# Attention and two layer pairs on one core: bias rows and transposes for two heads at a time, with a new order of the work

## The chip, the cores and the metric

The kernel runs on one core of a Trainium2 chip. Its engines are TensorE (PE, matmuls; PEld is its weight load), VectorE (DVE), ScalarE (ACT), GpSimd (POOL) and SyncE (SP), which here issues every DMA. The metric is the device time of one execution in microseconds (us); lower is better. The kernel before took 1053.97 us in the median of three runs (1053.57 to 1055.98).

## The reference

Batch 4, 8 heads, 576 positions, head size 64. The scores get a bias per head from a small network on the distance of two positions; softmax and the value product follow. The result, 2304 tokens of 512, goes through two layer pairs of 512 to 2048 to 512.

```python
scores = scale * np.matmul(q, k.transpose(0, 1, 3, 2))
x = (psi_rel / psi_i)[..., None]
bias = np.maximum(x @ w1 + b1, 0.0) @ w2            # one row per position and head
scores = scores + bias.transpose(2, 0, 1)[None]
attn = np.exp(scores - np.max(scores, axis=-1, keepdims=True))
attn = attn / (np.sum(attn, axis=-1, keepdims=True) + 1e-09)
x = np.matmul(attn, v)                              # then tokens x 512
h = x @ w_in; x = (s * np.maximum(h, 0.0) ** 2 + b) @ w_out
h = x @ w_in2; return (h - np.tanh(h)) @ w_out2
```

## The kernel before

**Precision.** Operands of the large matmuls are split into a high and a low f16 part, and three products are taken. So most data pass through a pair of steps: a copy to f16 ("hi") and the rest ("lo"). Layer weights of eight bytes are first converted by three VectorE instructions (L1253, L1256, L1259).

**Attention.** A unit is one head of 128 query rows of one batch, or two heads of the last 64 rows; there are 144, in groups of four that share an accumulator. For each unit (`unit_tasks`, `unit_rest`): one matmul group makes the scores of two heads (L1041); VectorE adds the bias row tile `bi` and takes the maximum (L1073); a small addition makes the exponent's offset (`mx_add`, L1081); ScalarE takes the exponential and its sum (L1087); `hi` copies it to f16 (L1099 on ScalarE, L1097 on VectorE); `lo` makes the low part in two pieces (`lo_a`, `lo_b`, L1104); a DMA transpose moves the 128 x 1152 tile `hl` into the 9 blocks of `et` (L1119); `pv` multiplies with the values (L1132, L1138). `x_tasks` scales a finished group and transposes it into the first layer's input (L1217, four blocks; L1220 for 64 rows).

**Bias.** For each of 36 blocks Q of 16 positions (`bias_tasks`) four hidden tiles are made (`hid`, L727 on ScalarE, L730 else; GpSimd only for Q < `QG`, which is 7), multiplied (L761), evacuated in two pieces into a tile of the `et` ring (`out`, L611, L615) and written to DRAM (`btd`). `bias_rows` reads them back skewed, one transfer for each head, into `bi`. Two batches share a load.

**Rings.** Each kind of tile has a fixed number of slots, handed out in order: `bi` 4, `hl` 3, `et` 4 (for heads and for bias rows on their way out), each for one head.

**Layers.** The first pair works on blocks of 256 tokens (`moe1_in`, L1573, L1645) from the moment four groups are through, beside the rest of attention. When attention is done (`turn`), its memory goes to the second pair's weights, which are converted, combined and split (L1852, L618) while TensorE works off the first pair; then the second pair runs (L2038, L2166).

**The order.** A planner (`Schedule.forward`) simulates engines and one DMA queue and emits the instructions in the order found. Each task has costs for the engines that may do it. `COST` multiplies them by kind, `XFER` scales transfers and gives their delay, `ENGINE` ties a task of a stage or group to engines (keys `u0` to `u9` are groups of four units), `SHIFT` moves its priority. `PORT` and `share` say whether it is kept from running beside GpSimd.

Of the kernel before, what the change touches and what calls it, by code (L numbers as in the profile page):

```python
# [8 lines left out]
F32 = mybir.dt.float32  # L9
F16 = mybir.dt.float16  # L10
# [16 lines left out]
SHARE0, QP, QA, SCU, QG = 21, 8, 16, 12, 7  # L27
# [3 lines left out]
AHEAD = 6.97  # L31
COST = {
    "u.ex@act": 0.848, "u.hi@act": 0.904, "bias.lambda@act": 1.1, "f.relu@act": 0.952, "f.square@act": 1.15,
    "x.lambda@act": 1.2, "w.lambda@act": 1.13, "scan.sq@act": 1.17, "bias.out@act": 1.0315, "f.out@act": 1.1149,
    "w.square@act": 1.07, "k.hi@act": 1.15, "s.lambda@act": 1.09, "q.hi@act": 1.2, "v.hi@act": 1.14,
    "u.ttr@dve": 0.84944, "f.hi@dve": 1.152216, "u.hi@dve": 0.87312, "s.in_done@dve": 1.1143, "scan.add@dve":
    0.8125, "f.lambda@dve": 1.174, "s.out_done@dve": 1.662, "u.lo@pool": 0.9991, "f.lo@pool": 0.782085,
    "bias.lambda@pool": 1.0466, "u.qk@pe": 0.885, "u.pv@pe": 0.97, "u.tr@sp": 1.04, "x.lambda@sp": 1.083,
    "q.fn@sp": 1.36, "J.c@dve": 1.2701, "J.fn@dve": 1.12, "L.lambda@dve": 1.0069, "L.square@act": 0.919,
    "P.wsum@dve": 1.0042, "X.scales@dve": 0.7943, "X.sums@dve": 1.21, "X.xsum@dve": 1.1245, "bias.lambda@dve":  # L40
    1.0453, "bias.out@dve": 1.179, "f.norm@dve": 1.2446, "f.out@dve": 1.0696, "f.scales@dve": 0.4404,
    "k.hi@dve": 1.1296, "k.lambda@dve": 1.047, "q.hi@dve": 1.1098, "s.lambda@dve": 1.0224, "scan.lambda@dve":
    0.857, "v.hi@dve": 1.738, "v.lambda@dve": 1.0251, "w.lambda@dve": 0.993, ".begin@dve": 0.784, ".lambda@dve":
    1.116, "L.scales@dve": 0.961, "L.sums@dve": 0.868, "X.lambda@act": 1.021, "X.lambda@dve": 1.023,
    "q.lambda@dve": 1.026, "w.scale_out@dve": 0.859, "u.lo@act": 0.97, "u.lo_a@act": 0.97, "u.lo_b@act": 0.97,
    "u.lo@dve": 0.97, "u.lo_a@dve": 0.97, "u.lo_b@dve": 0.97, "u.lo_a@pool": 0.97, "u.lo_b@pool": 0.97,
    "f.lo@act": 0.85, "f.lo@dve": 0.85, "f.hi@act": 1.04, "f.hi@pool": 1.04, "u.hi@pool": 0.8, "u.ex@dve": 0.8,
    "u.ex@pool": 0.8, "u.ttr@act": 0.8, "u.ttr@pool": 0.8,
}
XFER = {  # L50
    "bias.fn": (0.79893, 1.75), "f.fn": (1.5147, 1.23), "k.fn": (1.07019, 1.73), "q.fn": (1.05633, 1.81),
    "scan.fn": (0.80982, 2.01), "u.fn": (1.21869, 1.21), "u.tr": (1.0197, 2.23), "v.fn": (0.97218, 2.27),
    "w.fn": (0.91872, 2.03), "x.fn": (1.188, 1.54), "x.lambda": (0.81873, 1.51), "L.fn": (0.87714, 2.6), "J.fn":
    (0.33264, 1.52), "X.fn": (1.54341, 1.41), "o.fn": (0.8514, 0.99), ".fn": (0.78903, 1.4),
# [10 lines left out]
    "dve", "u12.lo_a": "pool", "u12.lo_b": "pool", "u13.lo_a": "pool", "u13.lo_b": "pool", "u17.lo_b": "pool",  # L65
# [12 lines left out]
    "act", "X7.lambda": "act", "x5.hi": "dve", "x12.hi": "dve", "I3.lambda": "act", "u1.lo_b": "pool",  # L78
# [4 lines left out]
    "dve", "X3.lambda": "dve",  # L83
# [4 lines left out]
    ".begin": 158.6, ".eye": 204.2, ".fn": -49.3, ".lambda": 60.6, "I0.add": 1197.4, "I0.fn": -551.5,  # L88
# [324 lines left out]
def tile_kernel(  # L413
# [318 lines left out]
    def bias_tasks(Q):  # L732
# [1594 lines left out]
```

## Time and profile before

| | us |
|---|---|
| median of 3 runs | 1053.97 |
| profiled execution | 1057.96 |
| its span | 1056.2 |
| TensorE busy | 964.1 (91%) |
| VectorE busy | 881.6 (83%) |
| ScalarE busy | 667.5 (63%) |
| GpSimd busy | 250.1 (24%) |

The span runs from the first to the last instruction; the profiled execution's own time is 1.8 us longer. Shares of busy time are means over stages that have different limits: GpSimd works in the first 600 us alone, and TensorE is at 99% in the last third. Matmuls overlap one another in the trace, so the busy time of TensorE is no measure of its peak. Where a line is a helper's, such as L468 (plain DMAs) or L618 (low parts), the tile names tell the step.

### The profile page before, as it was taken

Reading aid. Unit: us, or ns where it says so; the run is one execution under the profiler, and the core shown is the slowest. Engines: PE = TensorE matmul, PEld = TensorE weight load, DVE = VectorE, ACT = ScalarE, POOL = GpSimd, SP = SyncE. Lnnn points to the kernel's source line nnn. Section 1 sums busy time; section 2 is a strip of 40 time slices with the busy share of each in tenths; the row PEclk is TensorE's granted clock in tenths of the full one; section 3 lists DMA queues with packets and bytes.
Section 4 is the critical chain, followed back from the end, with each engine's and each line's share of the span. In section 5 each row is a group of like instructions: output and inputs, shape, how many; then the busy total and the mean of one; then the engine's idle time right before and its main releaser. Section 6 shows DMA issues by size and latency. Waiting matters only on the chain.

```text
span 1056.2 us, 32450 instructions
## 1 busy us (share of the span) xinstructions
PE 964.1 (91%) x13486; PEld 833.2 (79%) x13486; DVE 881.6 (83%) x1918; ACT 667.5 (63%) x1307; POOL 250.1 (24%) x319
## 2 busy tenths in 40 slices
PE   5676678999988999999997999988999999999998
PEld 3233356778767788788886888878999999999998
DVE  6999899876568677786774889999999999999885
ACT  4797659749767565776853687766554555464452
POOL 6146437247542334455511000000000000000000
PEclk9767679899999999999999999998999999999999
DMA  9969995899999879999896904410001100100000
GB/s 341 398 227 216 311 236 119 184 200 252 245 197 230 168 179 176 201 188 207 171 180 104 397 21 138 148 36 12 32 23 32 52 23 22 42 22 23 22 22 22
DMA packets 261444, 153.66 MB, mean 145 GB/s; under 512 B 197680, under 2 KB 229552, under 8 KB 261296
## 3 DMA queue, kind: packets, MB, share of 16 engines
q1 hardware_dynamic: 261296, 151.59, 59.1%
q8 instruction: 105, 1.72, 0.7%
q14 instruction: 43, 0.35, 0.1%
HBM read 84.03 MB, written 20.33 MB: 99 GB/s over the span
## 4 chain that ended last, share of the span: by engine, by line
PE 43%; DVE 9%; ACT 3%; DMA 2%; issue 2%; POOL 1%; SPq 0%; DVEq 0%; ACTq 0%; POOLq 0%
PE acc L2166 14%; PE pa L2038 9%; PE pb L2038 7%; PE po L1645 5%; PE ph L1573 4%; PE po L2166 2%; DMA et<-hl 2%; DVE w2big L1852 2%; DVE w2big L618 1%; PE sp L1041 1%; DVE w1big L618 1%; ACT e L1087 1%; POOL hl L1104 1%; PE xp L1132 1%; DVE hr L1603 1%
## 5 line engine op out<-in xcount | busy, mean ns | idle before, releaser
L1645 PE MATMUL po<-hr,w1big 128*128 128x256 f16 x1728 | 202.9, 274 | 3.6 <-ACT x L1664 2.7
L1104 POOL TENSOR_TENSOR hl<-e,hl 128x64 f16<-128x64 f32 (+1 forms) x200 | 160.2, 818 | 184.9 <-ACT hl L1099 107.2
L1573 PEld LDWEIGHTS <-w1big 128*128 128x128 f16 x1728 | 166.9, 99 | 31.5 <-issue 10.6
L1645 PEld LDWEIGHTS <-w1big 128*128 128x128 f16 x1728 | 165.5, 98 | 26.5 <-issue 7.1
L2038 PEld LDWEIGHTS <-w2big 128*128 128x128 f16 x3024 | 175.2, 99 | 2.2 <-issue 2.1
L2166 PEld LDWEIGHTS <-w1big 128*128 128x128 f16 x3024 | 172.8, 98 | 0.0
L1087 ACT ACTIVATE e<-sp,mx 128x576 f32<-128x576 f32 x144 | 105.6, 735 | 70.3 <-POOL mx L1081 34.3
L1073 DVE CUSTOM_DVE_ANT_0 sp<-sp,bi 128x576 f32<-128x576 f32 x144 | 107.0, 772 | 20.2 <-PE sp L1041 16.2
L1573 PE MATMUL ph<-xt_own,w1big 128*128 128x256 f16 x960 | 113.1, 274 | 3.0 <-ACT r L1586 2.2
L1041 PE MATMUL sp<-ks,qs 64*128 64x288 f16 (+1 forms) x960 | 84.2, 296 | 25.8 <-ACT e L1087 24.8
L1573 PE MATMUL ph<-w1big 128*128 128x256 f16 x768 | 91.2, 276 | 3.3 <-ACT r L1586 2.6
L1041 PEld LDWEIGHTS <-qs 64*128 64x128 f16 (+1 forms) x960 | 48.7, 99 | 53.0 <-issue 42.2
L1132 PEld LDWEIGHTS <-et 128*128 128x128 f16 (+1 forms) x1440 | 54.7, 104 | 41.2 <-issue 21.5
L1132 PE MATMUL xp<-vp,et 128*128 128x64 f16 (+1 forms) x1440 | 65.4, 199 | 19.1 <-DMA et<-hl 11.7
L2166 PE MATMUL acc<-hr,w1big 128*128 128x128 f16 x1296 | 79.9, 219 | 0.0
L1099 ACT ACTIVATE hl<-e 128x576 f16<-128x576 f32 x96 | 64.7, 678 | 23.1 <-DMA et<-hl 20.2
L2166 PE MATMUL acc<-w2big,w1big 128*128 128x128 f16 x1296 | 79.0, 219 | 0.0
L1104 DVE TENSOR_TENSOR hl<-e,hl 128x512 f16<-128x512 f32 (+1 forms) x88 | 48.8, 572 | 15.9 <-ACT hl L1099 13.0
L2038 PE MATMUL pa<-w1big,w2big 128*128 128x128 f16 x960 | 59.9, 219 | 1.7 <-ACT w2big L2057 0.9
L1586 ACT ACTIVATE r<-ph 128x512 f32<-128x512 f32 x72 | 42.3, 590 | 25.8 <-PE ph L1573 21.3
L1591 ACT ACTIVATE r<-r,sq 128x512 f32<-128x512 f32 x72 | 51.2, 718 | 0.9
L2074 ACT ACTIVATE w1big<-w1big 128x512 f32<-128x512 f32 x34 | 21.3, 630 | 45.6 <-DVE w1big L2064 33.4
(229 smaller groups left out, 1757.7 us busy)
## 6 DMA issues: line engine op xcount, KB each, us to landing
bi<-btd SPq DMA_DIRECT2D x64, 288.0 KB, 4.1
w1big<-in_wout SPq DMA_DIRECT2D x12, 1024.0 KB, 6.0
btd<-et SPq DMA_DIRECT2D x36, 295.5 KB, 3.7
w1big<-in_win SPq DMA_DIRECT2D x8, 1024.0 KB, 9.7
w2big<-in_win SPq DMA_DIRECT2D x8, 1024.0 KB, 13.1
x2d<-x SPq DMA_DIRECT2D x36, 128.0 KB, 3.1
w1big<-x2d SPq DMA_DIRECT2D x36, 128.0 KB, 2.3
outT<-xt_own SPq DMA_DIRECT2D x18, 256.0 KB, 2.2
```

What stands on the lines that cost most here:

```text
L1041: nc.tensor.matmul(out=out, lhsT=qs.tile[64 * h:64 * h + 64, sq, p * r:p * r + r], rhs=ks.tile[64 * h:64 * h + 64, sk, half * HS:(half + 1 ...
L1073: nc.vector.tensor_tensor_reduce(out=st, in0=st, in1=bi.tile.rearrange("p (a b) -> p a b", a=2), scale=-1.0 / KAP, scalar=3.0e38, op0=ALU. ...
L1087: nc.scalar.activation(out=put(e, row_tile("e")).rearrange("p (a b) -> p a b", a=2), in_=sp.tile[:, :, 0:HS], func=AF.Exp, scale=-1.0, bia ...
L1099: nc.scalar.activation(out=h[:, 0:S], in_=e.tile, func=AF.Copy)
L1104: eng_of(eng).tensor_tensor(out=hl.tile[:, o:o + m], in0=e.tile[:, c:c + m], in1=hl.tile[:, c:c + m], op=ALU.subtract)
L1132: nc.tensor.matmul(out=xp[r0:r0 + r, o:o + 64], lhsT=et.tile[:, n, r0:r0 + r], rhs=vp.tile[:, 0, n % 5, 64 * h:64 * h + 64], start=n == 0, ...
L1573: nc.tensor.matmul(out=ph.tile[:, fi, :], lhsT=win_ap(1, sw, m, f), rhs=xa(sx, m), start=m == 0 and j == 0, stop=m == KM - 1 and j == 2,)
L1586: nc.scalar.activation(out=r.tile, in_=ph.tile, func=AF.Relu)
L1591: nc.scalar.activation(out=r.tile, in_=r.tile, func=AF.Square, scale=sq[:, fp // 4:fp // 4 + 1])
L1645: nc.tensor.matmul(out=po.tile[:, :NB1], lhsT=wout_ap(1, sw, f, c), rhs=rhl[f // 8][:, f % 8, sr, :], start=f == 0 and j == 0, stop=f == K ...
L2038: nc.tensor.matmul(out=bank.tile[:, f * HT:(f + 1) * HT], lhsT=w[:, sw, m, f * 128:(f + 1) * 128], rhs=xs[:, sx, m], start=p in (1, 2, 5) ...
L2166: nc.tensor.matmul(out=bank.tile[:, o + c * HT:o + (c + 1) * HT], lhsT=w[:, sw, f, c * 128:(c + 1) * 128], rhs=g[:, sx, f], start=new and ...
```

## The change

- Bias rows: `bi` holds two heads, one transfer loads both (for 64 rows two transfers, each with one half of two units); the ring has 2 slots.
- Exponentials: `hl` and `et` hold two heads, rings of 2 slots. The transpose is issued once for a pair, 18 blocks, when the low parts of both are done; both value products follow it.
- Two bias blocks share one `et` slot, each with its own write to DRAM; the second's evacuation comes after the first's.
- Further engines: `mx_add` on ScalarE, relu of the first pair and the four-bank copies `E` of the second pair on VectorE, `hid` on GpSimd for all Q (`QG` 36).
- The identity for the weight norm's maximum and the maximum are two-byte.
- `COST`, `XFER`, `ENGINE`, `SHIFT` and some planner constants have new values, by which the order of all engines changes. An entry of `ENGINE` may name several engines.

```diff
-SHARE0, QP, QA, SCU, QG = 21, 8, 16, 12, 7
+SHARE0, QP, QA, SCU, QG = 21, 8, 16, 12, 36
...
-    "u.ex@act": 0.848, "u.hi@act": 0.904, "bias.lambda@act": 1.1, "f.relu@act": 0.952, "f.square@act": 1.15,
+    "u.ex@act": 1.0706, "u.hi@act": 1.1865, "bias.lambda@act": 1.1, "f.relu@act": 0.952, "f.square@act": 1.15,
...
-    ROWS = dict(bi=4, e=2, hl=3, et=4)
+    ROWS = dict(e=2, hl=2, et=2)
...
-        ("bi", 4), ("e", 2), ("hl", 3), ("et", 4), ("stg", 4), ("qst", 1), ("qs", 2), ("ks", 8), ("vp", 8), ("s", 2), ("x", 1),
+        ("bi", 2), ("e", 2), ("hl", 2), ("et", 2), ("stg", 4), ("qst", 1), ("qs", 2), ("ks", 8), ("vp", 8), ("s", 2), ("x", 1),
...
-    eye32 = const.tile([128, 128], F32, name="eye32")
+    eye16 = const.tile([128, 128], BF16, name="eye16")
...
-        ev = inst("et")
+        ev = ev_of[Q] = ev_of[Q - 1] if Q % 2 else inst("et")
+        eo = Q % 2 * (S + 16)
...
+        t_ev = [sc.add(
+            {ACT: 0.87, DVE: 0.80}, out, t_bmm[Q] + (t_evs[Q - 1] if Q % 2 else []), d, [] if Q % 2 else [ev], [i, ev]
+        )]
...
+        rows = btd[it][o:o + r * (H * BW - 1)].rearrange("(i c) -> i c", c=H * BW - 1)
+        return rows[:, :2 * step * BW].rearrange("i (a c) -> i a c", a=2)[:, :, :S]
...
+        elif k % 2:
+            t_bi[u], bi_of[u] = t_bi[u - 1], bi_of[u - 1]
...
-                t_bi[u] = load(lambda: put(bi, row_tile("bi")), bias_rows(it, 2 * p + a), 0.93, deps, d - 8, [bi], after=prev)
+                t_bi[u] = load(lambda: put(bi, pair()), bias_rows(it, 2 * p, 1), 1.86, deps, d - 8, [bi], after=prev)
...
-        t_mx = sc.add({DVE: 0.16, POOL: 0.3}, mx_add, [t_ttr[u]], d + 1.5)
+        t_mx = sc.add({DVE: 0.16, POOL: 0.31, ACT: 0.2}, mx_add, [t_ttr[u]], d + 1.5)
...
+        if not odd:
+            return
+
         def tr(_):
             nc.sync.dma_start_transpose(
                 out=put(et, row_tile("et", F16).rearrange("p (n r) -> p n r", r=128)), in_=hl.tile
             )
-        t_tr[u] = sc.add({SP: (1.25, 1.4)}, tr, t_lo, d + 5 - 500, [et], [hl])
+        t_tr[u] = t_tr[u - 1] = sc.add({SP: (1.4, 2.8)}, tr, t_los[u - 1] + t_lo, d + 5 - 500, [et], [hl])
+        for v in (u - 1, u):
+            unit_pv(v)
...
-            tr = sc.add({ACT: 0.21 + 0.8e-3 * 2 * w}, relu, tp + [t_bs], ready - 400, [r], [ph])
+            tr = sc.add(
+                {ACT: 0.21 + 0.8e-3 * 2 * w, DVE: 0.12 + 1.05e-3 * 2 * w}, relu, tp + [t_bs], ready - 400, [r], [ph],
+                share=0.0,
+            )
```

Of the `ENGINE` table the prediction speaks of these entries (of the others that it names there was none before):

```diff
-    "u4.mx_add": "dve", "u4.lo_a": "pool"
+    "u4.mx_add": "pool", "u4.lo_a": "dve", "u3.hi": "act", "u4.hi": "act", "u0.lo_a": "pool"
```

## Rows read from the trace of the kernel before

**Rows 1.** Busy us of PE, PEld, DVE, ACT, POOL by stage; granted clock; DMA share; GB/s.
```profile
0.00:60.00 60.00, 36.43 (x306) 17.67 (x310) 49.89 (x98) 40.77 (x73) 21.29 (x13) 0.81 0.99 374
60.00:153.00 93.00, 60.85 (x629) 35.30 (x621) 87.21 (x181) 66.24 (x146) 45.63 (x47) 0.72 0.91 237
153.00:200.00 47.00, 42.82 (x578) 31.84 (x578) 42.87 (x95) 41.19 (x84) 26.57 (x21) 0.93 0.76 154
200.00:572.00 372.00, 356.83 (x4807) 296.44 (x4803) 265.68 (x732) 248.07 (x562) 155.94 (x238) 1.00 0.98 195
572.00:721.00 149.00, 136.11 (x1308) 121.00 (x1307) 132.64 (x209) 105.58 (x196) 0.67 (x1) 0.98 0.39 134
721.00:1056.00 335.00, 331.09 (x5871) 330.92 (x5870) 303.33 (x610) 165.66 (x249) 0.00 (x0) 0.99 0.09 28
```

**Rows 2.** Waits of TensorE before 153 us: total, times, longest.
```profile
PE sp L1041 <- ACT e L1087: 16.3, 17, 2.6
...
PE xp L1132 <- DMA et<-hl: 6.1, 5, 1.9
```

**Rows 3.** Timeline, 144 to 154 us: start, duration, engine, line.
```profile
146.55 1.79 SPq L1217 DMA_TRANSPOSE xt_own<-xh  x1
...
153.47 0.71 PE L1573 MATMUL ph<-xt_own,w1big 128*128 128x256 f16 x5
```

**Rows 4.** Chain of waits, 560 to 725 us: shares by line.
```profile
by line: PE po L1645 22.7%; PE ph L1573 10.7%; DVE w2big L1852 9.8%; DVE w2big L618 8.9%; DVE w1big L618 7.1%; issue 5.1%; DVE w2big L1259 4.8%; DVE w2big L1256 4.3%; DVE hr L1603 3.7%; DMA et<-hl 3.1%; DMA w1big<-x2d 2.7%; PE pb L2038 2.4%
```

**Rows 5.** Output transposes of 4 blocks (L1217): min, median, max ns; landing us.
```profile
L1217 SPq DMA_TRANSPOSE xt_own<-xh x16: 1189/1220/2143, 92.6 to 556.7; - x16
...
DMA to landing us min/median/max: 2.5/3.8/5.6
```

**Rows 6.** Transposes of exponentials (L1119), 200 to 572 us, same columns.
```profile
L1119 SPq DMA_TRANSPOSE et<-hl x112: 1241/1358/3795, 199.3 to 566.1; - x112
...
DMA to landing us min/median/max: 3.2/4.0/8.1
```

**Rows 7.** Transposes of exponentials (L1119), 60 to 153 us.
```profile
L1119 SPq DMA_TRANSPOSE et<-hl x22: 1241/1442/4232, 66.6 to 151.5; - x22
...
DMA to landing us min/median/max: 3.2/5.3/9.0
```

**Rows 8.** Timeline of SP, 458 to 466 us.
```profile
459.00 6.30 SPq L1119 DMA_TRANSPOSE et<-hl  x4
```

**Rows 9.** DMA issues of the whole run: KB each, median us to landing.
```profile
bi<-btd SPq DMA_DIRECT2D x64, 288.0 KB, 4.1
...
bi<-btd SPq DMA_DIRECT2D x16, 144.0 KB, 3.0
```

**Rows 10.** Costliest groups of the page: exponential and its f16 copy on ScalarE.
```profile
L1087 ACT ACTIVATE e<-sp,mx 128x576 f32<-128x576 f32 x144 | 105.6, 735 | 70.3 <-POOL mx L1081 34.3
...
L1099 ACT ACTIVATE hl<-e 128x576 f16<-128x576 f32 x96 | 64.7, 678 | 23.1 <-DMA et<-hl 20.2
```

**Rows 11.** Groups of VectorE, 60 to 153 us: busy us, mean ns, idle before.
```profile
L1104 DVE TENSOR_TENSOR hl<-e,hl 128x512 f16<-128x512 f32 (+1 forms) x9 | 4.8, 544 | 0.7 <-ACT hl L1099 0.4 <-DMA et<-hl 0.2
...
L1097 DVE CAST hl<-e 128x576 f16<-128x576 f32 x4 | 3.2, 795 | 0.0
...
L1081 DVE TENSOR_SCALAR mx<-mx 128x1 f32<-128x1 f32 x20 | 2.8, 147 | 0.1
```

**Rows 12.** Groups of GpSimd before 60 us.
```profile
L730 POOL TENSOR_SCALAR hr<-u_sb,cst_sb 128x512 f32<-128x512 f32 (+5 forms) x8 | 20.8, 2608 | 9.4 <-PE pb L761 5.2 <-DVE u_sb L701 4.0 <-DVE qkc L824 0.2
```

**Rows 13.** Matmuls with the identity (tile eye).
```profile
L1341 PE MATMUL pm<-eye,wr x4: 421/488/582, 58.4 to 83.3; 128*128 128x128 f32 x4
```

**Rows 14.** Waits of TensorE, 200 to 572 us.
```profile
PE sp L1041 <- ACT e L1087: 6.6, 10, 2.3
PE xp L1132 <- DMA et<-hl: 5.6, 6, 2.5
```

**Rows 15.** DMA issues, 60 to 153 us.
```profile
btd<-et SPq DMA_DIRECT2D x13, 295.5 KB, 2.8
```

More of the change, by code (lines that the diff above doesn't have):

```diff
@@ L30 @@
 WI0, WI1, WO0, WO1 = 27.23, 74.31, 71.56, 137.63
-AHEAD = 6.97
+AHEAD = 7.0
 COST = {
-    "u.ex@act": 0.848, "u.hi@act": 0.904, "bias.lambda@act": 1.1, "f.relu@act": 0.952, "f.square@act": 1.15,
+    "u.ex@act": 1.0706, "u.hi@act": 1.1865, "bias.lambda@act": 1.1, "f.relu@act": 0.952, "f.square@act": 1.15,
     "x.lambda@act": 1.2, "w.lambda@act": 1.13, "scan.sq@act": 1.17, "bias.out@act": 1.0315, "f.out@act": 1.1149,
     "w.square@act": 1.07, "k.hi@act": 1.15, "s.lambda@act": 1.09, "q.hi@act": 1.2, "v.hi@act": 1.14,
[L36 to L48, printed above, removed]
@@ new lines @@
+    "u.ttr@dve": 0.966238, "f.hi@dve": 1.1079, "u.hi@dve": 1.24908, "s.in_done@dve": 1.1143, "scan.add@dve":
+    1.0563, "f.lambda@dve": 1.3736, "s.out_done@dve": 1.662, "u.lo@pool": 1.1227, "f.lo@pool": 0.763683,
+    "u.qk@pe": 0.885, "u.pv@pe": 0.97, "u.tr@sp": 1.04, "x.lambda@sp": 1.083, "q.fn@sp": 1.36, "J.c@dve":
+    1.2701, "J.fn@dve": 1.12, "L.lambda@dve": 1.0069, "L.square@act": 0.919, "P.wsum@dve": 1.0042,
+    "X.scales@dve": 0.7943, "X.sums@dve": 1.21, "X.xsum@dve": 1.1245, "bias.lambda@dve": 1.0453, "bias.out@dve":
@@ L286, in add @@
         only = ENGINE.get(t.key) or ONLY.get(kind)
+        if only is not None and not any(e in only for e in opts):
+            only = None
         t.opts = {}
@@ L346, in forward @@
                         at = max(at, port["pool"] - self.LEAD)
-                    elif eng == "pool" and t.opts[eng] < self.LONG:
+                    elif eng == "pool" and t.share > 0.0 and t.opts[eng] < self.LONG:
                         at = max(at, port["dve"] - self.LEAD)
@@ L390, in forward @@
             else:
-                if eng == "pool" and cost < self.LONG or eng == "dve" and t.share > 0.0:
+                if t.share > 0.0 and (eng == "pool" and cost < self.LONG or eng == "dve"):
                     port[eng] = at + cost
@@ L768, in out @@
             m = 16 * Q + 15
-            o = put(ev, row_tile("et"))
+            o = (ev.tile if Q % 2 else put(ev, row_tile("et")))[:, eo:]
             c = pinv_sb[:, Q:Q + 1]
@@ L1013, in unit_tasks @@
             deps = [t_bw[Q] for Q in range(8 * it, min(8 * it + 8, NQ))]
-            prev = [t_bi.get(u - 1)]
+            prev = [t_bi.get(u - 2 if k else u - 5)]
+            pair = lambda: row_p.tile([128, 2, S], F32, tag="bi", name="bi", bufs=2)
             if full:
-                t_bi[u] = load(lambda: put(bi, row_tile("bi")), bias_rows(it, 2 * p + a), 0.93, deps, d - 8, [bi], after=prev)
+                t_bi[u] = load(lambda: put(bi, pair()), bias_rows(it, 2 * p, 1), 1.86, deps, d - 8, [bi], after=prev)
             else:
-                ta = load(
-                    lambda: put(bi, row_tile("bi"))[0:64], bias_rows(it, 2 * p), 0.47, deps, d - 8, [bi], after=prev
+                ta = load(lambda: put(bi, pair())[0:64], bias_rows(it, 2 * p, 2), 0.94, deps, d - 8, [bi], after=prev)
+                t_bi[u] = load(
+                    lambda: bi.tile[64:128], bias_rows(it, 2 * p + 1, 2), 0.94, deps, d - 8, [], [bi], after=[ta]
                 )
-                t_bi[u] = load(lambda: bi.tile[64:128], bias_rows(it, 2 * p + 1), 0.47, deps, d - 8, [], [bi], after=[ta])
         bi = bi_of[u]
@@ L1080, in mx_add @@
             m = mx["m"]
-            eng_of(eng).tensor_scalar(out=m, in0=m, scalar1=LN_E, scalar2=None, op0=ALU.add)
-        t_mx = sc.add({DVE: 0.16, POOL: 0.3}, mx_add, [t_ttr[u]], d + 1.5)
+            if eng == ACT:
+                nc.scalar.activation(out=m, in_=m, func=AF.Copy, bias=LN_E)
+            else:
+                eng_of(eng).tensor_scalar(out=m, in0=m, scalar1=LN_E, scalar2=None, op0=ALU.add)
+        t_mx = sc.add({DVE: 0.16, POOL: 0.31, ACT: 0.2}, mx_add, [t_ttr[u]], d + 1.5)
         def ex(_):
@@ L1094, in hi @@
         def hi(eng):
-            h = put(hl, row_tile("hl", F16))
+            h = (hl.tile if odd else put(hl, row_tile("hl", F16)))[:, h0:h0 + S]
             if eng == DVE:
-                nc.vector.tensor_copy(out=h[:, 0:S], in_=e.tile)
+                nc.vector.tensor_copy(out=h, in_=e.tile)
             else:
-                nc.scalar.activation(out=h[:, 0:S], in_=e.tile, func=AF.Copy)
-        t_hi = sc.add({ACT: 0.60, DVE: 0.42}, hi, [t_exp[u]], d + 3, [hl], [e])
+                nc.scalar.activation(out=h, in_=e.tile, func=AF.Copy)
+        t_hi = t_his[u] = sc.add(
+            {ACT: 0.60, DVE: 0.42}, hi, [t_exp[u]] + ([t_his[u - 1]] if odd else []), d + 3, [] if odd else [hl], [e, hl]
+        )
         def lo(eng, part):
@@ L1104, in lo @@
             eng_of(eng).tensor_tensor(
-                out=hl.tile[:, o:o + m], in0=e.tile[:, c:c + m], in1=hl.tile[:, c:c + m], op=ALU.subtract
+                out=hl.tile[:, h0 + o:h0 + o + m], in0=e.tile[:, c:c + m], in1=hl.tile[:, h0 + c:h0 + c + m],
+                op=ALU.subtract,
             )
@@ L1121, in tr, with unit_pv @@
             )
-        t_tr[u] = sc.add({SP: (1.25, 1.4)}, tr, t_lo, d + 5 - 500, [et], [hl])
+        t_tr[u] = t_tr[u - 1] = sc.add({SP: (1.4, 2.8)}, tr, t_los[u - 1] + t_lo, d + 5 - 500, [et], [hl])
+        for v in (u - 1, u):
+            unit_pv(v)
+    def unit_pv(u):
+        sc.tag = f"u{u // 4 if u < 40 else 10 + u // 16}"
+        b, it, p, a, col = unit_of(u)
+        n, k = u // NP, u % NP
+        full = rows_of[it] == 128
+        et, vp, xp_i = et_of[u], vp_t[b, p], xp_of[n]
+        e0 = k % 2 * 9
         def pv(_):
@@ L1142, in unit_rest @@
         t_pv[u] = sc.add(
-            {PE: 0.42 if full else 0.85}, pv, [t_tr[u], t_vlo[b, p], t_pv.get(u - 1)], d + 10 - 1000,
+            {PE: 0.42 if full else 0.85}, pv, [t_tr[u], t_vlo[b, p], t_pv.get(u - 1)], tau(u) + 10 - 1000,
             [xp_i] if k == 0 else [], [et, vp, xp_i],
@@ L1340, in mm @@
             put(pm, ps_h.tile([128, 512], F32, tag="h", name="pm")[:, :128])
-            nc.tensor.matmul(out=pm.tile, lhsT=m.to_broadcast([128, 128]), rhs=eye32, start=True, stop=True)
+            nc.tensor.matmul(out=pm.tile, lhsT=m.to_broadcast([128, 128]), rhs=eye16, start=True, stop=True)
         t = sc.add({PE: 0.5}, mm, [t, t_eye], prio - 500, [pm])
@@ L1582, in moe1_in, with relu @@
             last = tp[-1:]
[L1584 removed]
+            def relu(e, fp=fp, ph=ph, r=r):
                 put(r, r_p.tile([128, 2, NB1], F32, tag="r", name="r")[:, :, :w])
[L1586 to L1587 removed]
+                if e == DVE:
+                    nc.vector.tensor_scalar(out=r.tile, in0=ph.tile, scalar1=0.0, scalar2=None, op0=ALU.max)
+                else:
+                    nc.scalar.activation(out=r.tile, in_=ph.tile, func=AF.Relu)
+            tr = sc.add(
+                {ACT: 0.21 + 0.8e-3 * 2 * w, DVE: 0.12 + 1.05e-3 * 2 * w}, relu, tp + [t_bs], ready - 400, [r], [ph],
+                share=0.0,
+            )
             def square(_, fp=fp, r=r):
@@ L2056, in copy @@
             st["t", n] = sc.add(
-                {ACT: 0.68}, lambda _: nc.scalar.activation(out=home(i), in_=bank.tile, func=AF.Copy, scale=ich),
-                [t] + (first_use["E"] if k < 2 else []), pr - 300, [i], [bank],
+                {ACT: 0.68, DVE: 0.66}, lambda e: copy_scale(home(i), bank.tile, ich, e),
+                [t] + (first_use["E"] if k < 2 else []), pr - 300, [i], [bank], share=0.0,
             )
```

78 lines of the change are left out of this document (46 added, 32 removed), and 271 rows, old and new, of tables (ENGINE, SHIFT).

## The prediction

> **What bounds the kernel now.** I read the busy table by stage first. The stages are cut at the first head scores (60 us), the first matmul of the first layer pair (153), its saturation (200), the end of attention (572) and the moment from which the second layer pair never stops (721). The reader is to see two things [rows 1]. From 200 to 572 TensorE is busy 356.8 of 372 us at granted clock 1.00, so it is full, and its idle time is 15.2 us. From 721 on it is busy 331.1 of 335. There nothing can be won but by doing less TensorE work, and the change does no less. Its idle time lies in the rest: 23.6 us before 60, 32.2 us from 60 to 153, 4.2 us to 200, 12.9 us from 572 to 721. Together with the 15.2 and 3.9 this is the whole 92 us.
>
> [...] The stage ends when the four groups of 256 tokens are through: the last transpose of attention output goes out at 146.55, the first matmul of the layer starts at 153.47 [rows 3]. From then on TensorE always has filling work. So each us by which that start moves is a us of the end, as long as TensorE stays full behind it.
>
> After 572 the chain of waits holds VectorE's work on the second pair's weights (sums 9.8%, low parts 8.9 and 7.1%, conversions 4.8 and 4.3%) beside TensorE's backlog of the first pair (22.7 and 10.7%) [rows 4]. VectorE is busy 132.6 of 149 us there. So the end of attention counts too: it is the gun for this preparation.
>
> The profiled execution took 1057.96 us (span 1056.2), 3.99 us above the median of the three timed runs, 1053.97. I make the sum on the profiled one and carry the difference over.
>
> **The change part by part.** *Transposes for two heads.* 144 transfers of 9 blocks become 72 of 18. Issue: a 4-block transfer holds SP for at least 1.189 us (median 1.220) [rows 5], a 9-block one for at least 1.241 (median 1.358) [rows 6]; the five blocks more cost 0.05 to 0.14 us. So 18 blocks should hold SP about 1.61 us (1.358 and nine fifths of 0.14), with ends of 1.24 (as 9) and 2.72 (as two). Per pair 2 x 1.358 - 1.61 = 1.11 us of SP go, 62 us over the 56 pairs from 200 to 572, 12 us over the 11 before 153 [rows 6, 7]. That is time of a queue that hands out everything in order, but not time on the path after 200, where matmuls cover it.
>
> Landing: the minimum is 2.5 us for 4 blocks [rows 5] and 3.2 for 9 [rows 6], 0.14 us a block, so 18 blocks come 1.3 us later than 9; the ends are nothing, and the 5.3 us of the busy stage once more [rows 7]. I take 1.3, next to the four back-to-back issues of 6.30 us (1.58 each) [rows 8]. It is paid where nothing hides it, at the last pair before the first matmul at 153; at the last pair of attention the backlog of the first layers hides it. The first head of a pair now also waits for the high and low parts of the second; the second's would have been awaited anyway, since a group of four heads is closed by its last one. While SP stands at the pair's transpose for that low part, bias loads, bias writes and output transposes queue behind it, one head (some 3 us) longer than before at worst; the loads behind it belong to later heads, so only a load that was late already pays.
>
> [...]
>
> *Bias rows of two heads.* 80 loads become 40. A load of 144 KB lands in 3.0 us, one of 288 KB in 4.1 [rows 9]; with the same slope 576 KB take 6.3 us (ends 4.1 and 8.2). The slots hold the same four heads, but come free in twos, so the next load starts one head later. After 200 a head goes by every 372 / 112 = 3.3 us [rows 6], and two other heads lie between, 6.6 us: hardly more than 6.3. I put it at nothing before 200 and at +1 us after it, for the matmuls of the first layer stand behind every such wait.
>
> *Two slots for two heads, in place of three and four for one.* For the high and low parts there is more room (4 heads for 3). For the transposed tile the room is equal, but bias rows on their way out now take half the ring for two evacuations; this is the first rival.
>
> *Order and engines.* The planner's cost of an exponential was 0.78 x 0.848 = 0.66 us and becomes 0.835, that of the f16 copy on ScalarE 0.54 and becomes 0.71; the trace has 0.735 and 0.678 [rows 10]. So the old order was laid for a ScalarE faster than it is, and the new one is laid for one nearer the measured one. Up to 153 VectorE does 3.2 us of casts, 4.8 us of low parts and 2.8 us of small additions that others can do [rows 11]. The new table sends the casts of groups 3 and 4, open before, to ScalarE, the first low part of group 0, also open, to GpSimd, and the additions of group 4 from VectorE to GpSimd; it gives the first low part of group 4 back to VectorE. I take 4 of these 10.8 us as gone from the full engine (ends: none, and all). GpSimd may now do hidden rows of any block, but one costs it 2.61 us [rows 12]; nothing of it is on the path. What is late next before 153 is SP; its 12 us freed above should take a third off the 6.1 us that value products wait for transposes there [rows 2]: 2 us.
>
> *Small edits*, cost nothing: the identity in two-byte form serves four matmuls of 0.49 us [rows 13], none later than 84 us and off the path; relu and four-bank copies on VectorE are choices, which after 572 would add to the fuller engine (bound 3 us).
>
> Sum on the profiled execution. Before 153: -4 (VectorE) - 2 (SP) + 1.3 (last pair lands later) = -4.7. From 200 to 572: of the 12.2 us that scores and value products wait [rows 14] the freed queue takes 3 us, bias loads give 1 back: -2. From 572: the idle 12.9 us is a matter of order; I take a quarter, -3.2 (ends -10 and +6). Sum -9.9, so 1048.1 there and 1044 in the median.
>
> **The rivals.** *The transposed ring jams (slower).* From 60 to 153 there are 13 bias writes that land in 2.8 us [rows 15] and 22 transposes that land in 5.3 [rows 7]. Before, the four slots held 13 x 3.7 + 22 x 5.7 = 173 of 372 slot-us (with the planner's own 0.9 us to evacuate and 0.4 for a value product): 47%. Afterwards 6.5 pairs of bias rows hold some 8 us each (an estimate: two evacuations, the landing, and between them four hidden rows at ScalarE's planned 0.6 us and their matmuls) and 11 pairs of heads 5.3 + 1.3 + 0.8 = 7.4 us: 133 of 186, 72%, handed out in order. If each bias pair pushes the pair of heads behind it by half its hold, that is 6.5 x 4 = 26 us, and what the 8.5 us between pairs doesn't hide, half, is +13 before 153, in place of the -6: 1057.96 + 13 + 1.3 - 5.2 = 1067 there, 1063 in the median. It decides from a first matmul of the layer later than 160 us. For it: the share; against it: bias writes can be ordered in advance of the heads.
>
> *Nothing that counts is touched.* SP and DMA are eased where TensorE is full anyway, and VectorE's 4 us come back as waits for ScalarE. 1054, by two us either way. For it: TensorE is 96% busy from 200 to 572 [rows 1] and needs no faster attention there. Against it: the 12.9 and 32.2 us idle in two stages that the new order also lays anew.
>
> *Twice the gain.* If the freed queue lets the first 16 heads run without the waits of [rows 2] on transposes and exponentials (22.4 us together, half of it) and half of the 12.9 us after 572 goes, it is -11 - 6 - 4 = -21: 1033. For it: in that stage SP holds a transpose for 1.44 us and up to 4.2 us [rows 7] while all else queues behind it.
>
> **How the numbers follow.** Forecast (1038 to 1050) 0.41, twice the gain (below 1038) 0.18, nothing touched (1050 to 1057) 0.15, jam or another order fault (above 1057) 0.26. The likeliest case gives 1044 with its own range of 1038 to 1050. About 0.3%, 3.2 us, is what a measurement of this kernel can tell from no change, so the same is 1050.8 to 1057.1: 0.13; faster 0.60; slower 0.27. The range goes to 1030 and 1064, leaving a tenth on either side.
>
> **What would show it.** Right: 72 transposes with SP hold near 1.6 us and landing 1.3 us longer; first layer matmul near 149; VectorE less full from 60 to 153; second pair saturated by about 712. Wrong: an SP hold of 2.5 us or more (the blocks cost, not the transfer); evacuations or transposes that wait for a slot of the transposed ring; a first matmul after 153; a longer VectorE chain after the end of attention.

## The result and the profile after

The changed kernel takes 1066.18 us (median of four runs, 1064.42 to 1074.36) against 1053.96 of the kernel before on the same chip: ratio 1.0121, interval 1.0078 to 1.0164. It is slower; the forecast was 1044.

The first profile of it is of its slowest run (1074.36). The rows below are of a second one (e7, 1064.40, span 1062.4), set against a second one of the kernel before (e8, 1055.05, span 1053.3), both at the usual time of their kernel: 9.1 us of span to explain. First the stages of the changed kernel, cut as in [rows 1] at its own marks: busy us of PE, PEld, DVE, ACT and POOL, granted clock, DMA share, GB/s.

```profile
0.00:60.00 60.00, 37.63 (x309) 18.34 (x310) 44.43 (x92) 48.73 (x88) 26.13 (x16) 0.89 0.98 366
60.00:152.00 92.00, 59.63 (x597) 32.30 (x598) 83.97 (x155) 69.39 (x155) 55.47 (x49) 0.76 0.90 237
152.00:200.00 48.00, 43.28 (x633) 32.81 (x633) 45.12 (x104) 41.53 (x87) 25.81 (x30) 1.00 0.85 183
200.00:572.00 372.00, 351.69 (x4718) 289.37 (x4717) 258.06 (x697) 262.06 (x611) 151.85 (x202) 0.98 0.95 193
572.00:739.00 167.00, 153.35 (x1543) 138.27 (x1538) 150.02 (x250) 108.25 (x198) 8.58 (x6) 0.97 0.35 123
739.00:1062.00 323.00, 319.25 (x5703) 318.88 (x5699) 291.98 (x576) 158.77 (x238) 0.00 (x0) 1.00 0.09 28
```

The end of attention stays near 572, but TensorE now idles 20.3 us from 200 to 572 in place of the 15.2 of [rows 1] (13.4 in e8), at granted clock 0.98 in place of 1.00 (0.99 in e8), and the moment from which the second pair never stops moves from 721 to 739. The start of the first pair, in the timeline (start, duration, engine and line, idle time before it and who ended it), is 152.50, a us earlier than in [rows 3] and half a us earlier than in e8 (152.96):

```profile
152.50 0.71 PE L1613 MATMUL ph<-xt_own,w1big 128*128 128x256 f16 x5 [0.57 <-DVE na L1572]
```

The transposes of 18 blocks: SP hold in ns (min, median, max) and landing in us, to be read against [rows 6, 7]. Then the bias loads of 128 rows (against [rows 9]).

```profile
L1149 SPq DMA_TRANSPOSE et<-hl x72: 2425/3324/7842, 69.9 to 564.7; - x72
...
DMA to landing us min/median/max: 4.5/6.2/9.8
```

```profile
bi<-btd SPq DMA_DIRECT2D x32, 576.0 KB, 5.0
```

18 blocks hold SP for 3.32 us in the median, more than two issues of 9 blocks (2 x 1.36). They land 1.3 us later than 9 by the minimum, 2.2 by the median. The waits of TensorE from 200 to 572 (total, times, longest) show where it idles, beside [rows 14]; in e8 the value products wait 2.8 us for transposes and the scores 7.3 us for exponentials:

```profile
PE xp L1172 <- DMA et<-hl: 9.0, 9, 2.1
PE sp L1058 <- ACT e L1111: 6.2, 9, 1.4
```

The queue stands at these transposes for the low parts of GpSimd: 78.7 us, where the second profile of the kernel before has 28.2.

```profile
SPq L1149 <- POOL hl L1130: 78.7, 31, 4.7
```

```profile
SPq L1119 <- POOL hl L1104: 28.2, 29, 1.8
```

Now the 9.1 us. The last value product is 2.0 us later (571.9 against 569.9). From there to the end it is 490.50 us, first fence, against 483.40 in the kernel before, second fence (columns as in the stages): 7.1 us more, 6.4 of them TensorE busy, 0.7 idle.

```profile
571.90:1062.40 490.50, 472.70 (x7249) 457.25 (x7242) 442.10 (x825) 267.02 (x436) 8.58 (x6) 0.99 0.18 60
```

```profile
569.90:1053.30 483.40, 466.32 (x7200) 450.99 (x7194) 436.41 (x820) 270.93 (x445) 0.67 (x1) 0.99 0.18 60
```

TensorE has more to do there, because it got less done before: the groups of that stretch show 672 output matmuls of the first pair in the changed kernel and 624 in the other. These are 48 more; by their mean (76.5 us for 672) they take 5.5 us. Of the first layer both leave 480.

```profile
L1691 PE MATMUL po<-hr,w1big 128*128 128x256 f16 x672 | 76.5, 272 | 3.5 <-ACT x L1710 1.8 <-DVE hr L1649 0.9 <-DVE x L1705 0.8
```

```profile
L1645 PE MATMUL po<-hr,w1big 128*128 128x256 f16 x624 | 70.4, 273 | 2.9 <-ACT x L1664 2.6 <-DVE x L1659 0.3
```

So the end of attention alone misleads: the order kept attention nearly on time and paid with the first pair's work, which then stands behind it. Where the second pair starts there is a second difference: in the 40 us from the last matmul of the first pair on (at 712.6 and 701.8) the granted clock is 0.87 in place of 0.96, and 514 matmuls run in place of 574 (changed kernel first).

```profile
712.60:752.60 40.00, 33.23 (x514) 32.85 (x512) 39.11 (x52) 29.09 (x42) 0.00 (x0) 0.87 0.06 18
```

```profile
701.80:741.80 40.00, 34.22 (x574) 33.73 (x572) 39.00 (x66) 29.75 (x43) 0.00 (x0) 0.96 0.06 18
```

### The profile page after: what moved, and what is told of

It reads as the page before. It is cut to its first block, busy times and chain, and to the rows that moved or that the text cites. A ratio compares the mean times of both kernels' runs of the same rounds, so it can differ in the third digit from the quotient of the medians.

```text
span 1072.4 us, 32069 instructions
## 1 busy us (share of the span) xinstructions
PE 966.5 (90%) x13484; PEld 830.5 (77%) x13484; DVE 874.9 (82%) x1869; ACT 689.2 (64%) x1375; POOL 266.8 (25%) x300
## 4 chain that ended last, share of the span: by engine, by line
PE 49%; DVE 12%; DMA 12%; ACT 5%; issue 2%; SPq 2%; POOL 1%; DVEq 0%; ACTq 0%; POOLq 0%
PE acc L2212 12%; PE ph L1613 9%; PE pa L2084 8%; PE po L1691 6%; PE pb L2084 6%; DMA et<-hl 6%; PE sp L1058 2%; PE po L2212 2%; DMA bi<-btd 2%; PE xp L1172 2%; DMA qst<-in_qT 2%; DVE w2big L1296 1%; DVE w2big L1299 1%; ACT e L1111 1%; DVE w2big L625 1%
## 5 line engine op out<-in xcount | busy, mean ns | idle before, releaser
L1130 POOL TENSOR_TENSOR hl<-e,hl 128x64 f16<-128x64 f32 (+1 forms) x169 | 144.4, 870 | 150.4 <-ACT hl L1123 91.8
L1613 PE MATMUL ph<-xt_own,w1big 128*128 128x256 f16 x960 | 116.7, 280 | 2.8 <-ACT r L1629 2.5
L1130 DVE TENSOR_TENSOR hl<-e,hl 128x512 f16<-128x512 f32 (+1 forms) x119 | 67.0, 579 | 20.5 <-ACT hl L1123 16.9
L1123 ACT ACTIVATE hl<-e 128x576 f16<-128x576 f32 x104 | 69.3, 678 | 15.6 <-DMA et<-hl 15.0
L1172 PEld LDWEIGHTS <-et 128*128 128x128 f16 (+1 forms) x1440 | 52.0, 103 | 32.1 <-DMA et<-hl 21.9
L1649 POOL TENSOR_TENSOR hr<-r,hr 128x512 f16<-128x512 f32 x32 | 40.1, 1253 | 136.2 <-DVE hr L1643 116.0
L2084 PE MATMUL pa<-w1big,w2big 128*128 128x128 f16 x960 | 62.5, 224 | 3.3 <-ACT w1big L622 3.2
```

The costliest lines, as they stand in the source:

```text
L1123: nc.scalar.activation(out=h, in_=e.tile, func=AF.Copy)
L1130: eng_of(eng).tensor_tensor(out=hl.tile[:, h0 + o:h0 + o + m], in0=e.tile[:, c:c + m], in1=hl.tile[:, h0 + c:h0 + c + m], op=ALU.subtract,)
L1172: nc.tensor.matmul(out=xp[r0:r0 + r, o:o + 64], lhsT=et.tile[:, e0 + n, r0:r0 + r], rhs=vp.tile[:, 0, n % 5, 64 * h:64 * h + 64], start=n ...
L1613: nc.tensor.matmul(out=ph.tile[:, fi, :], lhsT=win_ap(1, sw, m, f), rhs=xa(sx, m), start=m == 0 and j == 0, stop=m == KM - 1 and j == 2,)
L1649: (nc.gpsimd if e == POOL else nc.vector).tensor_tensor(out=rh[:, :, 1, :], in0=r.tile, in1=rh[:, :, 0, :], op=ALU.subtract)
L2084: nc.tensor.matmul(out=bank.tile[:, f * HT:(f + 1) * HT], lhsT=w[:, sw, m, f * 128:(f + 1) * 128], rhs=xs[:, sx, m], start=p in (1, 2, 5) ...
```

## The experiments

Two questions: do the parts (paired transposes, paired bias loads, slots for two heads) cost, or the order that came with them? The first eight runs, e4 and e8 apart, keep the changed kernel's order and change a part or nothing; the rest, e15 apart, change the order. Times of different runs are compared by their ratios to the kernel before, which ran on the same chip each time.

**e1: 18 blocks issued as 9 and 9, same order.**

```diff
-            nc.sync.dma_start_transpose(
-                out=put(et, row_tile("et", F16).rearrange("p (n r) -> p n r", r=128)), in_=hl.tile
-            )
+            put(et, row_tile("et", F16).rearrange("p (n r) -> p n r", r=128))
+            nc.sync.dma_start_transpose(out=et.tile[:, 0:9], in_=hl.tile[:, 0:2 * S])
+            nc.sync.dma_start_transpose(out=et.tile[:, 9:18], in_=hl.tile[:, 2 * S:4 * S])
```

> The changed kernel in its own order; only each pair's transpose of 18 blocks is issued as two of 9 blocks, one right behind the other. Theory A (the cost goes with the blocks, merging saves the queue nothing): the two issues together hold SP as long as the one did (3.3 us median), time within 0.5% of the changed kernel's 1066, so 1061 to 1071. Theory B (merging saves issue time as I predicted, the loss is elsewhere): 72 more issues of over 1 us each are felt, 1075 or more. Theory C (one long transfer blocks the queue more than two short ones): 1058 or less.

1064.09 us, ratio 1.0079 (1.0048 to 1.0111). The two issues hold SP for 1391 and 1474 ns:

```profile
L1150 SPq DMA_TRANSPOSE et<-hl x72: 1241/1391/4499, 69.8 to 566.1; - x72
L1151 SPq DMA_TRANSPOSE et<-hl x72: 1257/1474/3979, 71.3 to 568.0; - x72
```

2.87 us in two against 3.32 in one: merging saves the queue nothing, it costs it about 0.5 us a pair. The time is theory A's, the hold is shorter than it said. Undoing the merge brings the ratio from 1.0121 to 1.0079, with intervals that overlap, so this is not most of the loss.

**e2: only the first head's 9 blocks are transposed, and both value products read them** (the second head's result is left out).

```diff
+            put(et, row_tile("et", F16).rearrange("p (n r) -> p n r", r=128))
+            nc.sync.dma_start_transpose(out=et.tile[:, 0:9], in_=hl.tile[:, 0:2 * S])
...
-        e0 = k % 2 * 9
+        e0 = 0
```

> The changed kernel in its own order, but only the first head's 9 blocks of each pair are transposed and both value products read them (it leaves out half of the transposed data). Theory A: SP holds fall to about 1.4 us a pair, and with the queue freed as the planner assumed, the time falls by at least 12 us, to 1054 or less. Theory D (the new order is itself the loss, on VectorE, ScalarE or TensorE): it stays at 1062 or more.

1041.83 us, ratio 0.987 (0.9847 to 0.9893), last value product at 550.3. In this order half of the transposes cost 2.5%, 26 us. I took it as proof that the order was not the loss; e15 shows that it was too early for that.

**e3: cuts of 10+8, 12+6, 14+4 and 16+2 blocks in turn, to read hold against size** (one run, 1080.17 us, above the 1060 to 1075 expected).

```diff
+            if j == 0:
+                nc.sync.dma_start_transpose(out=et.tile[:, 0:10], in_=hl.tile[:, 0:1280])
+                nc.sync.dma_start_transpose(out=et.tile[:, 10:18], in_=hl.tile[:, 1280:2304])
```

> The changed kernel, each pair's 18 blocks issued in two unequal pieces: 10+8, 12+6, 14+4, 16+2 in turn, one source line each. It measures how long SP is held for 2 to 16 blocks. Theory A: the minimum hold rises steadily above 9 blocks, some 0.13 us a block up to the 2.41 us minimum for 18. Rival: it is flat near 1.2 us up to a size and jumps only beyond it, so that a smaller merge would be free. Time not of interest, 1060 to 1075.

The first pieces, 10, 12, 14 and 16 blocks:

```profile
L1152 SPq DMA_TRANSPOSE et<-hl x18: 1252/1419/2571, 70.1 to 565.4; - x18
...
L1155 SPq DMA_TRANSPOSE et<-hl x18: 1297/1764/6207, 74.7 to 570.2; - x18
...
L1158 SPq DMA_TRANSPOSE et<-hl x18: 1305/2196/6540, 84.3 to 575.2; - x18
...
L1161 SPq DMA_TRANSPOSE et<-hl x18: 1792/3028/5747, 95.0 to 579.5; - x18
```

In the median the hold is flat up to some 10 blocks (1.22 to 1.42 us from 4 blocks on [rows 5]) and then rises to 3.03 at 16 and 3.32 at 18. The minimum stays flat longer, up to 14 blocks (1.31 us), and is 1.79 at 16 and 2.43 at 18: that is the shape of the rival, not theory A's steady rise. Whether the rise of the median at 12 and 14 is the size's own or other traffic's, the run does not separate. The slope between 4 and 9 blocks, from which the forecast went on, lies wholly in the flat part. (The second pieces, of 8, 6, 4 and 2 blocks, stand behind a long first one and hold 1380, 1598, 1690 and 1242 ns, so they don't measure their size alone.)

**e4: the changed parts with the tables and constants of the kernel before** (`COST`, `XFER`, `ENGINE`, `SHIFT`, `QG`, `AHEAD`, `PORT`, `HOP`); of the edit one line is shown.

```diff
-SHARE0, QP, QA, SCU, QG = 21, 8, 16, 12, 36
+SHARE0, QP, QA, SCU, QG = 21, 8, 16, 12, 7
```

> The changed kernel's tiles, rings and transfers, but the planner's tables and constants of before (costs, delays, engine choices, priorities). Theory A and the ring theory (two slots for pairs are coarser): the loss is in the structure, so 1066 or more, likely 1070 to 1085, since these priorities were not found for it. Theory D (the new order and engine choices are the loss): at or below 1060.

1093.53 us, ratio 1.0361 (1.0331 to 1.0391). It says less than I expected of it: tables searched for other parts give a poor order, so this does not measure the parts.

**e5: as e1, the first head's piece issued as soon as it is ready and its slot has been given out** (cut of the edit).

```diff
+        if not odd:
+            def first():
+                put(et, row_tile("et", F16).rearrange("p (n r) -> p n r", r=128))
+                nc.sync.dma_start_transpose(out=et.tile[:, 0:9], in_=hl.tile[:, 0:2 * S])
+            sc.early.append((et, t_lo, first))
+            return
```

> The changed kernel's order with the pair's transposes in two pieces of 9 blocks (as e1_split9), and the first head's piece issued as soon as its own low part is done and the slot is free (1.5 us earlier in the plan in the median), the second head's where the pair's was. Theory A (the loss up to the end of attention is that the first head waits for the second, and SP stands there): 1054 to 1060 us, value products wait for transposes under 3 us from 200 to 570, last value product before 570 us. Rival B (the waiting of the first head is hidden, the rest of the loss lies elsewhere): 1061 to 1067 us, as e1. Rival D (what is left of the loss comes after the end of attention, from the order of the weight preparation): the last value product moves, but from the first conversion of the second pair's weights to the end it still takes 475 to 476 us (469.8 in the kernel before).

1081.12 us, ratio 1.0228 (1.0203 to 1.0252): by the ratios 1.5% or 16 us worse than e1, against the times of theory A and rival B. Only the stretch that rival D named came as it said (475.3 us, below). Waits of the queue from 60 to 200 us (L1165 is the early piece):

```profile
SPq L1165 <- PE xp L1201: 21.5, 6, 9.3
```

The early piece stands 21.5 us for the value products that still read its slot. From 152 to 200 us 126 GB/s are moved, where e1 moves 181 (DMA share 0.59 against 0.89), and the first layer matmul comes at 157.7 (153.1 in e1). This is the jam of the transposed ring that the first rival described; it is there when pieces are issued early. In the changed kernel, which issues late, the same wait is 5.1 us from 60 to 200 (2.8 in the kernel before; first profiles of both). The last value product comes 14.2 us later than in e1, so most of the loss builds up after 200; how much of it is this wait was not measured.

**e6: as e1, each bias load of 128 rows as two of 288 KB** (cut of the edit).

```diff
+                    dma(bi.tile[:, 0], bias_rows(it, 2 * p, 1)[:, 0])
+                    dma(bi.tile[:, 1], bias_rows(it, 2 * p, 1)[:, 1])
```

> e1_split9 with every bias load of 128 rows issued as two of 288 KB into the same slot, same order. If one transfer of 576 KB in place of two is what costs (other transfers behind it for its whole length): 1055 to 1061 us. If it costs nothing or saves a little (the load lands in 4.8 us, SP spends 0.4 us more here): 1062 to 1068 us. Theory A and rival D both expect the second.

1063.8 us, ratio 1.0065 (1.0047 to 1.0083), as e1: the size of the bias load is worth nothing that shows. (That its slots come free in twos was not tested by itself.)

**e7 and e8: second profiles of the two kernels.** No edit.

> The changed kernel once more, for a second profile of it at its usual time. Rival D expects from the first conversion of the second pair's weights to the end 475 to 476 us again, whatever the end of attention does; the run-to-run difference then lies before. Theory A expects the last value product at 573 to 577 us (579.5 in the first profile, of a run 8 us above the median) and value products still waiting for transposes by 5 us or more from 200 to 570. SP hold of 18 blocks: 3.2 to 3.4 us in the median.

> The kernel before once more, for a second profile of it at its usual time. Rival D expects 469 to 471 us from the first conversion of the second pair's weights to the end. If instead this stretch is 474 us or more, the difference of 5.7 us after attention is chance of one run. Last value product at 567 to 572 us.

1064.40 and 1055.05 us. From the first conversion of the second pair's weights to the end (start of the first `w2big` conversion by VectorE, taken from the span) it is 475.8 us in both profiles of the changed kernel and 475.4, 475.7, 474.6, 475.3 and 475.1 in e1, e2, e3, e5 and e6, whose order is the same; 469.8 and 468.5 in the kernel before. So this stretch goes with the order, here some 6 us longer, and does not move with transposes or bias loads. It is no measure of the loss, though: in e12 and e14 below, both faster than the kernel before, it is 473.3 and 480.2 us. The last value product in e7, 571.9, came just before the 573 to 577 of theory A; its other marks came. In e8 the 468.5 is half a us below the 469 to 471 of rival D, and the last value product (569.9) came in its range.

**e9: the changed parts, order laid anew.** The planner is given 2.41 us of hold for 18 blocks, and the search over `SHIFT` and `ENGINE` by the planner's own forecast goes on. Of the edit only the hold is shown; the new tables are left out.

```diff
-    "u.tr@sp": 1.04
+    "u.tr@sp": 1.812030
```

> The changed kernel with only its order and engine choices laid anew: the planner is told that a transpose of 18 blocks holds the queue for 2.41 us (the lowest measured) in place of 1.38, and the search goes on from the changed kernel's tables until its own forecast is 1028.3 us (1050.6 with the tables as they were). Theory O (the order that came with the change was laid for a queue hold of 1.38 us and not searched to its end; the pairing itself costs little): 1036 to 1050 us. Theory S (the pairing itself costs: 18 blocks in one hold, slots for two heads): 1058 us or more. Rival M (what the planner gains does not reach the chip): 1055 to 1070 us, like the changed kernel.

1050.16 us, ratio 0.995 (0.9933 to 0.9968): 16 us from the changed kernel (18 by the ratios) with the same parts, of which casts, low parts and small additions may change their engine, and faster than the kernel before. It is at the upper edge of theory O. The planner had forecast a gain of 22.3 us. The hold of 18 blocks is 3413 ns in the median, no shorter.

**e10: bias loads paired, transposes of one head and an `et` slot for each bias block again; e11: the kernel before; both with orders searched on.** Cut of e10's edit:

```diff
-        ("bi", 2), ("e", 2), ("hl", 2), ("et", 2),
+        ("bi", 2), ("e", 2), ("hl", 4), ("et", 4),
...
-        t_tr[u] = t_tr[u - 1] = sc.add({SP: (1.4, 2.8)}, tr, t_los[u - 1] + t_lo, d + 5 - 500, [et], [hl])
+        t_tr[u] = sc.add({SP: (1.25, 1.4)}, tr, t_lo, d + 5 - 500, [et], [hl])
```

> The changed kernel with the transposes of one head again (9 blocks each, four slots of one head for the high and low parts and four for the transposed tile and the bias rows on their way out), bias loads for two heads kept, order searched anew under the same planner tables; its own forecast is 1026.7 us. Theory O: as e9 within 6 us. Theory S: 1036 to 1048 us, and e9 at least 10 us slower. If the paired bias loads are what costs: this one and e9 both 1056 us or more while e11 gains.

> The kernel before with its own tables and structure, order searched on for about as long; its own forecast falls from 1031.1 to 1023.6 us. Theory O: some of it reaches the chip, 1044 to 1053 us. Rival M: 1052 to 1060 us.

1055.68 us, ratio 0.9988 (0.996 to 1.0015), and 1052.69 us, ratio 0.9971 (0.9953 to 0.9989). Theory S expected e9 to be 10 us slower than e10; it is 5.5 faster. The 1052.69 of e11 lies in the ranges of theory O and of rival M; its interval says that a gain of some 3 us is there.

**e12: as e9, but the planner keeps its 1.38 us of hold** (tables only, nothing else differs from the changed kernel).

> The changed kernel, order searched on as long as for e9 but with the planner's hold of 1.38 us for 18 blocks left as it was; its own forecast falls to 1024.7 us, and the same order planned with a hold of 2.41 us is forecast at 1055.6. Theory H (the loss came from the queue hold that the planner was told): 1056 us or more. Theory L (it came from a search that was stopped too early, whatever the hold): 1045 to 1053 us, like e9.

1047.52 us, ratio 0.9916 (0.9886 to 0.9946). Theory H, which I held until here, falls: with a hold that is wrong by two us a pair (1.38 told, 3.48 in the median) the searched order is as good. What the changed kernel lacked was an order searched on, not a better hold in the planner: told 2.41 us, the planner puts e12 at 1055.6 and the changed kernel at 1050.6, and on the chip e12 is the faster by some 20 us. Two stretches of e12, from the last value product to the end and the 40 us from the last matmul of the first pair on (694.9):

```profile
555.10:1044.70 489.60, 475.19 (x7296) 459.26 (x7290) 445.35 (x827) 264.52 (x434) 8.96 (x7) 1.00 0.18 60
```

```profile
694.90:734.90 40.00, 34.71 (x583) 34.08 (x581) 39.05 (x65) 29.81 (x43) 0.00 (x0) 0.96 0.06 19
```

Attention ends 16.8 us earlier than in e7, and the stretch behind it is 0.9 us shorter, although 48 more matmuls of the first pair stand in it (648 of its second layer and 552 of its first, where e7 has 672 and 480). So nearly all of the gain lies before the end of attention. At the start of the second pair the clock is 0.96 again, and 583 matmuls run in place of 514. The wait of the queue for the low parts is no loss by itself: it is 74.3 us here from 200 to 555, nearly as long as in e7.

**e13: as e9, a second search; e14: as e10, a second search.** Orders only.

> As e9 (paired transposes, hold of 2.41 us), order from a second search of the same length with another seed, forecast 1028.9 us. If the gain of e9 is that of the pairing with an order that knows the hold: 1045 to 1054 us. If it was the luck of one order: 1055 us or more.

> As e10 (bias loads paired, transposes of one head), order from a second search, forecast 1024.9 us. If transposes for two heads are worth nothing in themselves: within 4 us of e13. If they gain: 1054 us or more, above e13. If they cost: under 1047 us.

1050.22 us, ratio 0.994 (0.992 to 0.996), and 1047.47 us, ratio 0.9925 (0.9902 to 0.9947). The gain of e9 is not the luck of one order. But the same parts with two orders, e10 and e14, lie 8 us apart (6.6 by the ratios), more than lies between the means of pairs (ratios 0.995, 0.994, 0.9916) and singles (0.9988, 0.9925). e14 is 2.8 us below e13 on the same chip, inside the 4 us that stood for "worth nothing" and half a us above the mark for a cost. What pairing the transposes is worth in itself stays open; these five orders put it within some 5 us of nothing.

**e15: e12 with half of the transposes**, the edit of e2 (the second head's result is left out).

> e12 (the changed kernel's parts and planner costs, order searched on) with only the first head's 9 blocks transposed, which both value products of the pair read; as e2_half did in the changed kernel's own order (1041.8, 24 us less). If the changed kernel's order lost because it left the transposes uncovered, and the searched one covers them: 1036 to 1045 us here, so e12 loses less than 10 us to them where the changed kernel lost 24. If the searched order is faster for other reasons: 1018 to 1030 us, again some 20 us less than e12.

1030.07 us. The ratio is 0.976 (0.9716 to 0.9805). By the ratios, halving saves 1.6% here and 2.5% in the changed kernel's order, 16 and 26 us of 1054. Between the two orders lie 2.05%, 21.6 us: by this sum some 10 are transposes that the first order left uncovered, some 12 are lost elsewhere in it (0.987 against 0.976, both with half). With the intervals of the ratios the 10 is good to some 8 us and the 12 to some 5. I had expected under 10 us here if the transposes were all of it, or some 20 if none; it is between, and nearer to none.

The stretch from 200 us to the last value product shows where the transposes cost, in e2, e12 and e15 (columns as in the stages; for e7 see the first table):

```profile
200.00:550.30 350.30, 342.61 (x4688) 284.26 (x4686) 249.00 (x694) 257.86 (x609) 150.82 (x201) 0.99 0.72 156
```

```profile
200.00:555.10 355.10, 340.90 (x4684) 282.24 (x4683) 273.94 (x704) 250.38 (x590) 148.74 (x212) 1.00 0.99 202
```

```profile
200.00:540.40 340.40, 338.13 (x4695) 281.88 (x4694) 273.42 (x708) 252.03 (x594) 149.11 (x213) 1.00 0.78 164
```

With half of the transposes the idle time of TensorE there falls from 20.3 us (e7) to 7.7 (e2) and from 14.2 (e12) to 2.3 (e15). The last value product comes 21.6 and 14.7 us earlier, while the first layer matmul moves from 152.5 to 150.0 and from 151.9 to 152.5. So transposes are on the path after 200 in both orders. The runs do not tell whether by the hold, by the landing or by the traffic, since all three are halved.

## Why the prediction was wrong

**The step that failed is the credit for the new order.** "The idle 12.9 us is a matter of order; I take a quarter, -3.2 (ends -10 and +6)" for the time from 572 on; it measured +7.1, beyond its own end. Of that, 5.5 us are the 48 matmuls that should have run before, so most of the loss is older: "-2" from 200 to 572 measured +2.5 (the last value product 2.0 us later, after a start half a us earlier), and +8.0 with these matmuls. "-4.7" before 153 measured -0.5 to -1.0 (first layer matmul at 152.50, before at 152.96 and 153.47). The three terms make -9.9 in the sum and +9.1 in the two profiles (-0.5, +2.5 and +7.1). e12 shows the cause with nothing but the tables changed: 1047.52 us with the same parts, so the order that came with the change costs about 20 us (18.7 by the medians, 21.6 by the ratios) against one that can be found. I had read single entries of the tables (casts, low parts, additions moved) as gains. They do not add up to a time: the order of all engines is one term, and for these parts alone it spans 1047 to 1066 us, and to 1093 us with the tables of the kernel before (e4).

**SP hold of 18 blocks**: 1.61 taken, ends 1.24 and 2.72; 2.43 at least and 3.32 in the median, past the upper end. The sign named as wrong ("the blocks cost, not the transfer") came true: the queue lost about 0.6 us a pair instead of gaining 1.11. So the 5 us that the sum credits to a freed queue (2 before 153, 3 after 200) had nothing to stand on. As a loss of its own the longer hold is small: e1 gets back 2 us by the medians, and e9 and e12 are fast with it.

**The overlap after 200.** The prediction says that time of the queue is not on the path there, "where matmuls cover it". e2 and e15 show that the transposes are: leaving half of them out is worth 2.5% in the changed kernel's order and 1.6% in that of e12, and in the profiles most of the gain comes behind the first layer matmul. It is that of hold, landing and traffic together.

**What held.** Landing 1.3 us later: 4.5 against 3.2 by the minimum (2.2 by the median). Bias loads land in 5.0 us where 6.3 was estimated, and e6 finds no price for their size, where +1 us was put. VectorE, the fullest engine of that stage in [rows 1], is less full from 60 to 152, by 2.3 us of the 4 taken (84.0 us against 86.3 in both profiles of the kernel before); the start came forward by less, so VectorE was not all that held it. Of the signs of being wrong, the longer stretch after the end of attention came as well (475.8 against 469.8 and 468.5 us), but e12 and e14 show that it does not tell a slow order from a fast one.

**The rivals.** The jam of the transposed ring, my slower one at 1063, names nearly the right time for the wrong reason: its own sign, a first layer matmul later than 160, did not come (152.50); e5 shows it in another order. "Another order fault", which stood beside it in its 0.26 without a mechanism or a size of its own, is what happened. The profile could not have told which order: but that the term was wide, and that its sign was not to be read from entries, could have been said, and the forecast should then have stayed near no change.

**Open.** Which places of the first order lose the 12 us that are not transposes, beyond the slow start of the second pair that its profile shows; whether transposes for two heads gain or cost once the order is equally good; and whether the new parts gain anything over the kernel before with an order searched as long, since e11 is a single order (0.9971, beside 0.9916 to 0.995 for the pairs) and two orders of the same parts differ by 0.6%. Half of the transposes in the order of the kernel before was not tried.

## What to carry to other kernels

Where a change brings a new order for everything, the order is a term of its own, and here it was wider than the parts (about 20 us against some 5): judge the parts with orders searched equally long, and take more than one. An extrapolated hold needs a point beyond the size in question: the flat piece here between 4 and 9 blocks (1.22 and 1.36 us in the median) said nothing of 18 (3.32). And read how much filler work stands behind a mark before trusting the mark: attention ended nearly on time here with 5.5 us of other work put off, and in e14 it ended 17.8 us earlier than in e13 for 7.1 us of span, with 120 more matmuls of the first pair behind it.

## What the chip showed that was not expected

In the median, one issue of a transpose held the queue about as long for 4 as for 10 blocks (1.2 to 1.4 us) and then longer: 1.76 at 12, 2.20 at 14, 3.03 at 16, 3.3 to 3.5 at 18. The minimum is 1.31 us up to 14, 1.79 at 16 and 2.43 at 18. Two issues of 9 are shorter together than one of 18 (2.87 against 3.32 us). Transfers that were issued early into slots still being read were worse than late ones: in e5 they stood 21.5 us from 60 to 200, the DMA share from 152 to 200 was 0.59 in place of 0.89, and the run was 1.5% longer than e1.
